# Seven products for all eight pairs of blocks, and one written order for eight batches

## The chip, the core and the metric

One core of a Trainium2 chip. Its engines take their instructions in order, each from its own queue: TensorE (PE; PEld is its weight load), VectorE (DVE), ScalarE (ACT), GpSimd (POOL) and SyncE (SP), which here issues nearly all transfers. The metric is the device time of one execution in microseconds.

## The reference

Two attentions per batch through 32 packed tokens, then a two-layer block with a gate. 8 batches, 8 heads, 576 rows, 64 per head, so 4608 tokens of 512; the hidden size is 2048.

```python
p_packed = sm_attn(p, k, v)             # 32 packed rows against 576 keys
out = sm_attn(q, p_packed, p_packed)    # 576 rows against the 32 packed rows
x = out.transpose(0, 2, 1, 3).reshape(B * S, H * D)
h = x @ w_in
g = h * np.clip(h + 3.0, 0.0, 6.0) / 6.0
return g @ w_out
```

## The kernel before

**Number form.** The large products are made as three matmuls each, of high and low parts in a 32-bit format: high by high, high by low, low by high (`product`, line 967). The low part is the value less its high part, made by a copy on ScalarE and a subtraction (`split`, line 945); `parted` (line 949) does that with the subtraction on GpSimd (line 947).

**First product.** The attention's second step is folded into the first layer: `u_m` multiplies the packed rows of a batch by a quarter of the first layer's weights (`M`, four quarters a batch), and `first_product` (line 922) makes the hidden rows of one of 16 blocks of 128 with six matmuls of 256 or 320 columns. `gate_into` (line 938) applies the gate: ScalarE's addition and cut (line 940), VectorE's minimum and product (line 941). First products use two banks of PSUM in turn (`ps_h`). A batch of 576 rows is two halves of 256 rows and 64 left-over rows, which the wide half (320 columns) keeps in `bnd` (line 965); the left-over rows of two batches make one more group of 128.

**Second product.** A block by itself (a single) is multiplied into both accumulators A and B of a half, three matmuls of 512 columns each. Two blocks together (a pair, `pair_product`) are a 2x2 product of block matrices in seven products instead of eight, 21 matmuls of 256 columns, with four accumulators A to D. The sums that it needs on the row side are made for each half (VectorE, lines 1241, 1249, 1254; parts by `parted`), those on the weight side, `T1` to `T4`, once in batch 1 (`combine`, line 1058). Six of the eight pairs take this form from batch 2 on, four in the second half of batch 1, none before. The combined weights have four places; pairs 0 and 1 share theirs with 4 and 5, and are kept in DRAM and fetched in turn (`fetch_t`, line 1104). After the last pair the four singles follow, and during them the sums of C and D are made (lines 1134 to 1146); the last single closes A and B (line 1153) and the half's two row blocks are stored. Left-over rows of batches 2 and 3 are joined to the singles of a half of batch 3; those of 4 to 7 make a half of their own in batch 7 (`moe_edges`).

**Attention of the next batch** runs in the gaps of the current one: `S` (scores of packed rows against keys, `u_s1`), `E`, `V`, `T`, and `Z` (scores of queries, `u_s2`). A round of scores is eight small matmuls packed into TensorE's array, one bank of PSUM for even and one for odd heads; 576 columns go as two rounds of 288, one after the other (`both_halves`, line 362), since one pair of banks serves the attention. Batch 1 alone has both rounds at once.

**Order.** Batch 0 runs by a list written by hand (`PLAN`): each name is a chain, each mention its next step. From batch 1 on, steps are handed to a planner, which orders them by simulated costs; `fill` (line 1449) hands out the attention's steps behind the gates of the current block, with counts in `STAGES`, `LATE`, `TURN` and `FETCHES`.

Of the kernel before, what the change touches and what calls it, by code (L numbers as in the profile page):

```python
# [18 lines left out]

STAGES = (((0, 1), (6, 2), (19, 2)), ((0, 1), (10, 2), (19, 1)))


LATE = (3, 2, 1, 2, 1)
PAIRS = 6
FIRST_PAIRS = 4
TURN = (
    (5, 5, 6, 6, 7, 7, 7), (7, 8, 8, 9, 9, 9, 10), (10, 10, 11, 11, 12, 12, 12), (13, 13, 13, 14, 14, 15, 15),  # L30
    (27, 27, 28, 28, 28, 29, 29), (29, 29, 30, 30, 30, 31, 31),
)
FETCHES = (((5, 1), (7, 0)), ((5, 4), (7, 5)))

PLAN = """
in in in in lo0 lo2 in in k0 in p li0 k1 in p k0 k2 k1 kr k2 in s0 kr b2 s0 b0 k3 s0 b2 li1 s0 warm b2 s0 in
k3 b2 in b0 s1 s0 li2 q1 b2 e0 q1 c0 s1 b2 e0 q0 c0 li3 s0 s1 v0 q0 s0 s1 s1 v0 b0 lp s1 b0 e1 a0 v0 c1 qr
v0 e1 c1 s1 a0 z0 qr b0 s1 a0 z0 b0 v1 a0 z0a a1 z0a upper a1 z0a lo1 q2 v1 li4 a1 q3 q2 z0a a1 v1 q3 v1 z0a  # L40
z1 z1 li7 a2 m0 z1a a2 m1 a2 z1a a2 lo3 a3 z1b z0a lk0 a3 z1b z1b z0a z1b z0a z1a z0a z1b lo5 z1a b1 li6 z1a
z1b m0 z1b b1 z1a z1a z1b z0a a4 z1a m0 li5 z1b z0a warm a3 z1b z0a m1 m0 z1b a7 lk2 z1a h0 m0 z1a m1 b1 a7
z1a b1 b3 h0 b3 lo4 b3 a3 warm r0 m1 a4 r0 b3 m2 lo8 tp h1 r0 m1 a7 y0 b1 h1 r0 m2 lo6 a4 x0 b1 r1 a4 x0 m2
m2 a6 r1 x0 a6 m2 h2 a7 tk0 r1 h2 y1 a5 lk3 r1 a5 x0 y1 a5 x1 r2 a6 a5 b5 x1 r2 b3 x1 tk2 r2 y0 h3 a6 b4 r2
lk1 h3 b4 b5 m4 x1 b3 r3 b4 li8 b5 m4 b4 li10 r3 x2 li9 m4 m4 x2 lo7 r3 m4 b5 below h4 b4 tk3 y3 b6 h4 b4 y3
lq1 y2 b6 x2 r3 b5 x2 b6 r4 tk1 x3 b6 b8 r4 x3 a8 b5 S a8 x3 a8 r4 y4 a8 S S S S x3 b8 y4 h5 a10 li11 r4 a10
lo9 h5 a10 a9 b8 lq3 x4 b8 r5 x4 b6 r5 S x4 y2 a10 r5 tq1 h6 lo10 b8 r5 lq2 h6 y5 a9 y5 S x4 a9 r6 b8 x5 a9
S b7 S x5 r6 a11 x5 li12 S a11 a11 h7 b6 r6 a11 S h7 r6 x5 b9 r7 li13 m8 S lv b7 b7 x6 r7 y6 b7 m8 x6 y7 r7
# [27 lines left out]
def packed_attention_moe(  # L78
# [97 lines left out]

# [1338 lines left out]
```

## Time and profile before

| | us |
|---|---|
| median of 3 runs | 708.94 |
| lowest, highest | 706.88, 710.05 |
| profiled execution | 709.52 |
| its span, first to last instruction | 707.7 |

Busy time counts an engine's instructions alone; matmuls overlap, so the time of one on the page is longer than the distance to the next. A wait is put down to what ended last. The chain that ended last is, by share of the span, TensorE 82%, VectorE 7%, transfers 5%.

### The profile page before, as it was taken

To read this page: it belongs to the slowest core of one execution; us is meant where nothing else is said; L and a number is where in the kernel's file an instruction comes from. 1 tells how busy PE (TensorE), PEld (TensorE's weight loads), DVE (VectorE), ACT (ScalarE), POOL (GpSimd) and SP (SyncE) were. 2 spreads that over 40 slices of the span, in tenths; PEclk is the share of its full clock that TensorE was granted. 3 is DMA by queue.
4 is the path that set the end of the run, shared out by engine and by line. 5 is a ranking of instruction groups with operands and counts; after the bars stand their busy time and mean duration, and the time that the engine had idled before them with its cause. 6 is when DMAs were issued, how large, how long until landed. Compare 5 with 4: busy or idle time off the path is not lost.

```text
span 707.7 us, 16190 instructions
## 1 busy us (share of the span) xinstructions
PE 684.7 (97%) x5924; PEld 591.9 (84%) x5924; DVE 544.2 (77%) x1227; ACT 428.8 (61%) x1004; POOL 335.9 (47%) x515
## 2 busy tenths in 40 slices
PE   6599999999999999999999999999999999999997
PEld 4477877888879888899898888899888988899997
DVE  2897788788999759877788777877698778867754
ACT  5798876556566646565455655656475755565553
POOL 2475541113425456371272626474453646475552
PEclk9699999999999999999999999999999999999999
DMA  9989852955338655465554647375755644340330
GB/s 277 310 216 240 218 141 88 287 150 116 117 123 208 161 131 210 127 158 108 107 200 125 164 103 232 121 158 129 196 200 143 168 127 150 129 170 1 120 119 30
DMA packets 199679, 111.15 MB, mean 157 GB/s; under 512 B 173489, under 2 KB 185265, under 8 KB 195761
## 3 DMA queue, kind: packets, MB, share of 16 engines
q1 hardware_dynamic: 199056, 109.94, 55.8%
q8 instruction: 46, 0.75, 0.4%
q14 instruction: 33, 0.26, 0.1%
q10 hardware_dynamic: 544, 0.20, 0.1%
HBM read 92.27 MB, written 17.83 MB: 156 GB/s over the span
## 4 chain that ended last, share of the span: by engine, by line
PE 82%; DVE 7%; DMA 5%; issue 2%; SPq 1%; ACT 1%; POOL 1%; DVEq 0%; ACTq 0%; POOLq 0%
PE acc L969 48%; PE ps_hh L929 22%; PE ps L350 5%; PE ps_h L607 3%; DMA w_again<-w_kept 2%; PE ps L470 1%; SPq L294 1%; DMA room<-in_q_dram 1%; PE ps L440 1%; DMA wt<-t_kept 1%; DVE tr L555 1%; DMA p_nat<-in_p_dram 1%; DVE osb L1153 1%; PE ps L273 1%; DVE t L941 0%
## 5 line engine op out<-in xcount | busy, mean ns | idle before, releaser
L929 PE MATMUL ps_hh<-a_hi,m_hi 128*128 128x320 f32 (+1 forms) x448 | 133.5, 298 | 1.0 <-DVE t L941 0.9
L929 PE MATMUL ps_hh<-a_lo,m_hi 128*128 128x320 f32 (+1 forms) x448 | 133.0, 297 | 0.0
L929 PE MATMUL ps_hh<-a_hi,m_lo 128*128 128x320 f32 (+1 forms) x448 | 132.7, 296 | 0.0
L969 PE MATMUL acc<-wo_hi,g 128*128 128x512 f32 x304 | 109.0, 402 | 0.0
L940 ACT ACTIVATE t<-ps_hh,three 128x320 f32<-128x320 f32 (+1 forms) x148 | 73.5, 500 | 47.4 <-PE ps_hh L929 36.0
L941 DVE SCALAR_TENSOR_TENSOR t<-t,ps_hh 128x320 f32<-128x320 f32 (+1 forms) x148 | 65.7, 445 | 45.1 <-ACT t L940 44.4
L947 POOL TENSOR_TENSOR ge<-t,ge 128x256 fp32r<-128x256 f32 x76 | 60.3, 793 | 80.8 <-ACT ge L946 32.1
L929 PEld LDWEIGHTS ps_hh<-a_hi,m_hi 128*128 128x128 f32 x448 | 84.7, 189 | 7.7 <-DVE t L941 2.7
L929 PEld LDWEIGHTS ps_hh<-a_lo,m_hi 128*128 128x128 f32 x448 | 84.7, 189 | 4.8 <-issue 1.9
L929 PEld LDWEIGHTS ps_hh<-a_hi,m_lo 128*128 128x128 f32 x448 | 84.7, 189 | 1.7 <-issue 1.3
L965 POOL COPY bnd<-t 128x64 f32<-128x64 f32 x76 | 24.2, 318 | 120.0 <-DVE t L941 117.8
L969 PE MATMUL acc<-wt,ga 128*128 128x256 f32 x492 | 80.4, 284 | 0.3 <-ACT ga L946 0.2
L969 PE MATMUL acc<-wo_hi,ge 128*128 128x256 f32 x328 | 77.8, 285 | 0.0
L947 POOL TENSOR_TENSOR gf<-tb,gf 128x256 fp32r<-128x256 f32 x76 | 65.0, 855 | 17.5 <-ACT gf L946 14.9
L947 POOL TENSOR_TENSOR ga<-t,ga 128x256 fp32r<-128x256 f32 x76 | 60.8, 800 | 24.4 <-ACT ga L946 24.2
L969 PEld LDWEIGHTS acc<-wo_hi,g 128*128 128x128 f32 x304 | 56.1, 188 | 16.2 <-issue 3.0
L969 PEld LDWEIGHTS acc<-wt,ga 128*128 128x128 f32 x492 | 68.0, 190 | 1.2 <-issue 0.5
L969 PEld LDWEIGHTS acc<-wo_hi,ge 128*128 128x128 f32 x328 | 57.5, 190 | 7.0 <-issue 2.8
L969 PE MATMUL acc<-wo_lo,g 128*128 128x512 f32 x152 | 60.1, 395 | 0.0
L555 DVE STREAM_TRANSPOSE tr<-nat 128x576 f32<-128x576 f32 x56 | 42.4, 765 | 16.7 <-DMA nat<-in_q_dram 10.4
L940 ACT ACTIVATE tb<-ps_hh,three 128x256 f32<-128x256 f32 (+1 forms) x76 | 37.9, 499 | 23.0 <-PE ps_hh L929 18.6
L969 PE MATMUL acc<-wt,gf 128*128 128x256 f32 x246 | 50.1, 283 | 0.3 <-DMA wt<-t_kept 0.3
(234 smaller groups left out, 1780.5 us busy)
## 6 DMA issues: line engine op xcount, KB each, us to landing
w_again<-w_kept SPq DMA_DIRECT2D x24, 1024.0 KB, 4.8
wt<-t_kept SPq DMA_DIRECT2D x26, 768.0 KB, 5.2
out_dram<-osb SPq DMA_DIRECT2D x35, 256.0 KB, 2.4
nat<-in_k_dram SPq DMA_DIRECT2D x112, 72.0 KB, 3.2
nat<-in_q_dram SPq DMA_DIRECT2D x112, 72.0 KB, 2.7
raw_out<-in_moe_w_out_dram SPq DMA_DIRECT2D x10, 512.0 KB, 5.1
raw_in<-in_moe_w_in_dram SPq DMA_DIRECT2D x10, 512.0 KB, 5.6
w_kept<-w_in_sb SPq DMA_DIRECT2D x4, 1024.0 KB, 7.6
```

Of the source, the lines that this page charges most:

```text
L273: nc.tensor.matmul(banks[x][NPK * a:NPK * a + NPK, :n * P], state["pp"][half, NPAIR * x + a], cols[half, :, a], start=True, stop=True,)
L294: nc.sync.dma_start(out=t[r:r + 32], in_=src[b, 2 * a + h, :, 32 * c:32 * c + 32].rearrange("(t i) j -> i t j", i=32),)
L350: nc.tensor.matmul(pair[x][NPK * a:NPK * a + NPK, :n], rows[half, a], c, start=True, stop=True)
L440: nc.tensor.transpose(out=pair[x][:, c * P:(c + 1) * P], in_=e[x][:, c * P:(c + 1) * P], identity=ident)
L555: nc.vector.transpose(out=t, in_=state.pop(("nat", which, b, a)))
L607: nc.tensor.matmul(h[:, hf, :HS], mm[:, g, fs], aa[:, hf * HS:(hf + 1) * HS], start=(g == 0 and i == 0), stop=(g == NG - 1 and i == 2),)
L929: state["first"] = nc.tensor.matmul(h[:, :n], mm[:, g, fs], aa[:, t0:t0 + n], start=(g == 0 and i == 0), stop=(g == NG - 1 and i == 2),)
L940: state["relu"] = nc.scalar.activation(out=t[:, :n], in_=h, func=AF.Relu, bias=three)
L941: state["gate"] = nc.vector.scalar_tensor_tensor(out=t[:, :n], in0=t[:, :n], scalar=6.0, in1=h, op0=ALU.min, op1=ALU.mult)
L947: engine.tensor_sub(out=lo, in0=x, in1=hi.bitcast(F32))
L965: nc.gpsimd.tensor_copy(out=bnd[:, f, side * REM:side * REM + REM], in_=t[:, boff:boff + REM])
L969: nc.tensor.matmul(out, lhs[x], rhs[y], start=first and i == 0, stop=last and i == 2, skip_group_check=True)
```

## The change

- All eight pairs are made by seven products in batches 2 to 7 and in the half of left-over rows. In the first half of a batch they come in the order `DOWN`, in the second in `ORDER`; in batch 1 it stays four pairs. Combined weights of pair 3 and of pair 6 have places of their own, six others share three places, are kept in DRAM and fetched.
- Pair 6's place and a small staging tile take the room of `bnd`. So left-over rows of batches 2 to 6 go to DRAM, two blocks a store, and come back in batch 7, where those of 2 to 5 make a half and those of 6 and 7 a chain of their own.
- Scores from batch 2 on are one round of 512 and 64 columns. The 64 take both banks of the first products. Small transposes that took an accumulator's bank take the attention's.
- Batch 0's loads are chains of their own, and all eight batches run by written lists (`PLANS`), one step of one engine at a mention; `'` and `"` name a step of the batch before or after. Loads stand further ahead of their use, and queries and values ahead of the first output weights.
- In the last half, the sums of C and D and the last additions are cut in pieces of 256 columns on VectorE, each stored as it is made.

In the lists `f` is half of a first product, `g` the gate and the sums behind it, `a` to `d` the parts, `x` one of a pair's seven products, `e` the left-over rows, `r` and `o` the sums and stores of a half, `T` the combining of weights, `ft` a fetch; names with `n` belong to the next batch's attention (`nS`, `nZ` the scores). Shown are the first lines of batches 0 and 1, the lines around the scores in batch 2, and the last lines.

```diff
-LATE = (3, 2, 1, 2, 1)
-PAIRS = 6
...
+PAIRS = 8
 FIRST_PAIRS = 4
...
+ORDER = (1, 0, 2, 3, 5, 4, 6, 7)
+DOWN = (5, 4, 3, 7, 6, 1, 0, 2)
+
+SLOT = {0: 0, 1: 1, 2: 2, 3: 3, 4: 0, 5: 1, 7: 2}
+KEPT = {0: 0, 1: 1, 2: 2, 4: 3, 5: 4, 7: 5}
...
+PLANS = (
+    """
+lp0 lk_0 k0 lkr p p k0 lk_1 k1 k2 k1 s0 k2 lq_1 kr k3 k3 lqr kr s0 s0 s0 li0 lq_0 a0 a0 s0 s0 warm a0 s1 s1 q1
+s1 s1 s1 s1 e0 e0 c0 c0 q0 lv_0 v0 q1 q0 s0 s0 v0 s1 s1 e1 v0 c1 c1 lq_2 v0 qr qr a0 z0 z0 z0a z0a z0a li1 a1 e1
+q2 lv_1 a1 z0a z0a a1 a1 v1 v1 lq_3 q3 v1 v1 z0a q2 q3 z1 z1 z0a m0 z0a z0a lo2 b2 lo0 li2 b2 m0 upper z1b lp
...
+f00 'y14 f00 g00 'o1 nlk0 ntk0 M1 g00 nlk1 'x14 p00 p00 f01 f01 M2 M2 ntk1 M2 g01 g01 M2 f02 M2 ntp 'x15 f02 p01
+x00 e00 g02 g02 e01 p01 f03 p02 p02 nlk2 nlk3 f03 g03 g03 M3 T0 ntk2 ntk3 e03 p03 T0 x01 f04 j01 'o0 T0 M3 M3
...
+f05 f05 nlk3 f04 g01 d01 g04 d01 g03 c03 M3 x01 x01 x01 g03 c03 x01 a02 x03 x03 x01 g04 f06 M3 M3 f06 'T6 x03
+g05 g05 x03 x03 x03 d03 ntk3 g04 g06 g06 g05 c05 g05 a04 b05 d03 'T6 g06 nS nS nS f07 f07 b05 x05 x05 nS x03 a06
...
+d1d d1d f1f f1f x1b g1e x1b g1f g1f x1d x1b g1f g1f c1d d1b x1d x1d x1d o20 a1e a1e b1f b1f x1f ft12 x1f x1f x1f
+c1f c1f x1b x1d x1d d1f d1f x1b x1f x1f r1 x1d r1 x1f o10 r1 r1 o10 r1 o11 o10 o10 o11 o11
...
+def written(ch):
+
+    for b, plan in enumerate(PLANS):
+        for name in plan.split():
+            near = {"'": b - 1, '"': b + 1}.get(name[0])
+            yield (b, name) if near is None else (near, name[1:])
...
     def att_ps():
-        return spare_ps(0) if steady else ps_a.tile([P, 512], F32, name="ps1", tag="att")
+        return att_pair()[0] if steady else ps_a.tile([P, 512], F32, name="ps1", tag="att")
...
     def spare_pair():
         if steady:
-            return [spare_ps(x) for x in range(2)]
+            return [ps_h.tile([P, 512], F32, name="ps_s", tag="h") for _ in range(2)]
...
+    def all_rows(b, lhs, rhs):
+
+        cuts = (slice(0, HS), slice(HS, S)) if b == 1 else (slice(0, NB), slice(NB, S))
+
+        def cols(cut):
+            return lambda a, half: rhs[a][half].rearrange("p t i -> p (t i)")[:, cut]
+
+        done = each_head(lhs, *(cols(cut) for cut in cuts))
+        yield None
+        for n in (1, 0):
+            yield n, cuts[n], [ps[:, :cuts[n].stop - cuts[n].start] for ps in done[n]]
...
-        for part in both_halves(b == 1, pt, kt):
+        for part in all_rows(b, pt, kt):
...
-        for part in both_halves(not roles, pps[b % 2], qt):
+        for part in all_rows(b, pps[b % 2], qt):
...
+        if i == 6:
+            t6 = ep.tile([P, 3, 2, H2], F32R, name="wt6", tag="bnd0")
+            for k, name in enumerate(("T1", "T2", "T4")):
+                blocks[i, name] = [t6[:, k, x] for x in range(2)]
+            x, y = (stage8().rearrange("p f n -> p (f n)")[:, k * H2:(k + 1) * H2] for k in range(2))
...
+        if i in KEPT:
+            nc.sync.dma_start(out=t_kept[KEPT[i]], in_=slots[SLOT[i]].rearrange("p a x m -> p (a x m)"))
+            yield
+
+    def fetch_t(i):
+        nc.sync.dma_start(out=slots[SLOT[i]].rearrange("p a x m -> p (a x m)"), in_=t_kept[KEPT[i]])
...
+    def steps_of(b, c):
+
+        pairs = list(range(FIRST_PAIRS) if b == 1 else DOWN if c == 0 or b == LAST else ORDER)
+        return pairs, [2 * i + k for i in pairs for k in range(2)] + [
+            f for f in range(NF) if f // 2 not in pairs
+        ]
...
+    def keep_edge(b, keep, f, boff, side):
+
+        cols = slice(side * REM, side * REM + REM)
+        if b == 1:
+            place = bnd_at(f, 1)[:, 0, cols]
+        elif b == LAST:
+            place = parked["last"][f // 4][:, f % 4, cols]
+        else:
+            place = stage8()[:, f % 8]
+        nc.gpsimd.tensor_copy(out=place, in_=keep["t"][:, boff:boff + REM])
+        yield
+        if 1 < b < LAST and f % 2:
+            two = slice(f - 1, f + 1)
+            nc.sync.dma_start(out=e_kept[b // 2, :, two, cols], in_=stage8()[:, f % 8 - 1:f % 8 + 1])
+            yield
...
                     bank(x)[:, half * H2:half * H2 + H2], lhs[l], block(i, r), fresh,
-                    i == pairs[-1] and x in "CD",
+                    i == pairs[-1] and (x in "CD" or not singles),
...
+        def summed():
+
+            sixth = 1.0 / 6.0
+            r1, r2 = made["r"] = [gp.tile([P, DM], F32, name="osb") for _ in range(2)]
+            nc.scalar.activation(out=r1, in_=bank("C"), func=AF.Copy, scale=sixth)
+            yield
+            u1 = r2[:, H2:]
+            (nc.vector if end else nc.gpsimd).tensor_tensor(out=u1, in0=r1[:, :H2], in1=r1[:, H2:], op=ALU.add)
+            yield
...
+        def finished(k):
+            r = made["r"][k]
+            for cut in ((slice(0, H2), slice(H2, DM)), (slice(H2, DM), slice(0, H2)))[k] if end else (slice(0, DM),):
+                own = cut if k == 0 or singles else slice(cut.start, min(cut.stop, H2))
+                if own.start < own.stop:
                     nc.vector.scalar_tensor_tensor(
-                        out=dst, in0=bank("D")[:, half * H2:half * H2 + H2], scalar=sixth, in1=other,
-                        op0=ALU.mult, op1=ALU.add,
+                        out=r[:, own], in0=bank("AB"[k])[:, own], scalar=1.0 / 6.0, in1=r[:, own], op0=ALU.mult, op1=ALU.add
                     )
-
-                added(r1[:, H2:], 0, u1)
-                added(r2[:, :H2], 1, u1)
-                added(r2[:, H2:], 0, r2[:, :H2])
...
-        for name in PLAN.split():
+        for b, name in written(ch):
```

## Rows read from the trace of the kernel before

**Rows 1.** The page: busy time of each engine over the span, and TensorE's busy share and granted clock in 40 equal slices.

```profile
PE 684.7 (97%) x5924; PEld 591.9 (84%) x5924; DVE 544.2 (77%) x1227; ACT 428.8 (61%) x1004; POOL 335.9 (47%) x515
...
PE   6599999999999999999999999999999999999997
...
PEclk9699999999999999999999999999999999999999
```

**Rows 2.** TensorE's own waits over the whole span: what waited for what, us in total, times, the longest.

```profile
PE ps_t L886 <- DVE m_lo L286: 5.3, 1, 5.3
...
PE ps_w L803 <- issue: 2.0, 1, 2.0
...
PE ps_hh L929 <- DVE t L941: 0.9, 2, 0.5
PE ps L350 <- DMA w_again<-w_kept: 0.8, 1, 0.8
```

**Rows 3.** The timeline of TensorE at 400 to 412 us: start, duration, operation. Between the first two lines lie eleven starts of the same shape, between the last two three of 512 columns.

```profile
400.74 0.28 PE L929 MATMUL ps_hh<-a_hi,m_hi 128*128 128x256 f32 x1
...
402.18 0.28 PE L969 MATMUL acc<-wo_hi,gf 128*128 128x256 f32 x1
...
410.64 0.39 PE L969 MATMUL acc<-wo_hi,g 128*128 128x512 f32 x1
...
411.57 0.28 PE L929 MATMUL ps_hh<-a_hi,m_hi 128*128 128x256 f32 x1
```

**Rows 4.** The timeline of TensorE around score rounds: two rounds together in batch 1, a single round of a later batch, and a packed step of batch 0 with 32 columns.

```profile
10.04 0.30 PE L731 MATMUL ps_w<-room 64*32 64x32 f32 x16
...
55.85 0.39 PE L969 MATMUL acc<-wo_hi,gl 128*128 128x512 f32 x1
56.17 0.71 PE L350 MATMUL ps_w<-tr,p_tr 64*32 64x288 f32 x16
56.68 0.69 PE L350 MATMUL ps<-tr,p_tr 64*32 64x288 f32 x16
...
57.64 0.40 PE L969 MATMUL acc<-wo_lo,gh 128*128 128x512 f32 x1
...
476.41 0.31 PE L929 MATMUL ps_hh<-a_lo,m_hi 128*128 128x320 f32 x1
...
477.00 0.31 PE L929 MATMUL ps_hh<-a_hi,m_lo 128*128 128x320 f32 x1
477.24 0.71 PE L350 MATMUL ps<-tr,p_tr 64*32 64x288 f32 x16
...
478.11 0.28 PE L969 MATMUL acc<-wo_lo,gf 128*128 128x256 f32 x1
```

**Rows 5.** The timeline of all engines near the end: the last matmul of the last first product, and the end of its gate on VectorE (it comes by ScalarE, line 940).

```profile
699.39 0.28 PE L929 MATMUL ps_hh<-a_hi,m_lo 128*128 128x256 f32 x1
...
700.28 0.42 DVE L941 SCALAR_TENSOR_TENSOR t<-t,ps_hh 128x256 f32<-128x256 f32 x1 [0.37 <-ACT t L940]
```

**Rows 6.** Groups by line and shape on VectorE (busy us, mean ns, idle before); then two lines' operations with their shortest, median and longest duration in ns; the subtractions of line 947 on VectorE and GpSimd over the span; and two stretches with the busy time of each engine.

```profile
L1249 DVE TENSOR_TENSOR t<-t,tb 128x256 f32<-128x256 f32 x76 | 43.5, 572 | 1.5
...
L1254 DVE TENSOR_TENSOR tb<-tb,t 128x128 f32<-128x128 f32 x76 | 36.8, 484 | 1.6
...
L947 DVE TENSOR_TENSOR g<-t,g 128x256 fp32r<-128x256 f32 x72 | 30.1, 423 | 6.4 <-ACT g L946 4.7 <-PE acc L969 0.5
...
L1241 DVE TENSOR_TENSOR t<-t 128x128 f32<-128x128 f32 x76 | 24.6, 323 | 1.9
...
L1249 DVE TENSOR_TENSOR t<-t,tb x76: 400/426/965, 174.5 to 691.9; 128x256 f32<-128x256 f32 x76
...
L941 DVE SCALAR_TENSOR_TENSOR t<-t,ps_hh x148: 374/442/489, 121.5 to 700.3; 128x320 f32<-128x320 f32 x76, 128x256 f32<-128x256 f32 x72
...
0.00:708.00 708.00, 41.03 (x102) 227.62 (x322) 0.99 0.56 157
...
180.00:200.00 20.00, 18.85 (x163) 14.97 (x162) 19.03 (x40) 11.98 (x29) 9.56 (x13) 1.00 0.19 68
...
240.00:260.00 20.00, 20.00 (x217) 17.90 (x216) 13.88 (x39) 12.14 (x30) 7.78 (x14) 1.00 0.58 136
```

**Rows 7.** One stretch of the start with the busy time of each engine, granted clock, share of the DMA engines and GB/s; and the transfers that SyncE issued at the start.

```profile
20.00:40.00 20.00, 11.28 (x133) 8.51 (x133) 16.58 (x40) 14.52 (x30) 11.60 (x10) 0.66 1.08 295
...
1.77 0.50 SPq L176 DMA_DIRECT2D raw_out<-in_moe_w_out_dram  x1
2.31 0.60 SPq L176 DMA_DIRECT2D raw<-in_moe_w_out_dram  x1
...
4.79 0.90 SPq L643 DMA_DIRECT2D room<-in_q_dram  x2
```

**Rows 8.** The timeline of all engines at the end: the last two additions and the last matmul; and the copy of a bank that stands ahead of the sums, by shape.

```profile
703.22 1.39 DVE L1153 SCALAR_TENSOR_TENSOR osb<-acc,osb 128x512 f32<-128x512 f32 x2 [1.62 <-PE acc L969]
...
703.48 0.39 PE L969 MATMUL acc<-wo_hi,g 128*128 128x512 f32 x1
...
L1134 ACT ACTIVATE osb<-acc 128x512 f32<-128x512 f32 x14 | 8.4, 597 | 2.1 <-PE acc L969 2.0
```

**Rows 9.** SyncE's queue: its longest wait on a load of the attention inputs (in total, times, longest); and the page's line of block fetches (count, KB each, us to landing).

```profile
SPq L294 <- DVE tr L555: 67.2, 12, 8.8
...
wt<-t_kept SPq DMA_DIRECT2D x26, 768.0 KB, 5.2
```

More of the change, by code (lines that the diff above doesn't have):

```diff
@@ L44 @@
[L44 to L48, printed above, removed]
@@ L1109, in sums_of @@
+    def sums_of(ch, b, c, pairs, singles, rows):
         banks, made = {}, {}
+        end = (b, c) == (LAST, 1)
         def bank(x):
@@ L1127, in pair_product @@
                     bank(x)[:, half * H2:half * H2 + H2], lhs[l], block(i, r), fresh,
[L1128 removed]
+                    i == pairs[-1] and (x in "CD" or not singles),
                 )
[L1130 to L1138 removed]
+                yield
@@ new lines, in single_products @@
+        def single_products(f, keep):
+            g = keep["g"]
+            for k, x in enumerate("AB"):
+                second_product(
+                    f, bank(x), g[:, k * P:(k + 1) * P], g[:, (2 + k) * P:(3 + k) * P],
+                    first=False, last=f == singles[-1],
+                )
+                yield
+        def finished(k):
[3 more added lines that the diff above has]
+                if own.start < own.stop:
@@ L1204, in moe_pairs, with pairs_half @@
+                nc.sync.dma_start(out=rows[k][:, cut], in_=r[:, cut])
+                yield
+        ch[b, f"r{c}"] = summed()
+        for k in range(2):
+            ch[b, f"o{c}{k}"] = finished(k)
+        return pair_products, single_products
+    def pairs_half(ch, b, c):
+        pairs, steps = steps_of(b, c)
         even = b % 2 == 0
@@ L1284, in moe_pairs, with gate_even @@
-        if joined:
-            pend[-1:-1] = edges
+        pair_products, single_products = sums_of(
+            ch, b, c, pairs, steps[2 * len(pairs):], [out[row + k * P:row + (k + 1) * P] for k in range(2)]
+        )
+        def gate_even(keep):
+            ta = keep["t"] = gp.tile([P, WT], F32, name="t")
+            yield from gate_into(ta, keep, n)
+            a1, a2 = (ta[:, off + k * P:off + (k + 1) * P] for k in range(2))
+            nc.vector.tensor_sub(out=ta[:, W + off:W + off + P], in0=a2, in1=a1)
+            yield
@@ new lines, in last_edges, with acc, parts, products @@
+    def last_edges(ch, b):
+        banks = []
+        def acc():
+            if not banks:
+                banks.append(acc_of(roles[3]))
+            return banks[0]
+        for f in range(0, NF, 2):
+            summed, keep = f // 2 in ORDER, {}
+            def parts(f=f, summed=summed, keep=keep):
+                yield from edge_parts(edge_rows("last", f, 2), summed, keep)
+            def products(f=f, summed=summed, keep=keep):
+                yield from edge_product(acc, f, *keep["j"], summed, f == 0, f == NF - 2)
+            ch[b, f"j3{f:x}"] = parts()
+            ch[b, f"y3{f:x}"] = products()
+        ch[b, "o30"] = stored(acc, out[b * S - REM:b * S + REM], dict(tag="g", bufs=4))
@@ L1490, in packed_attention_moe @@
-            if (b, c) == (FOUR + 3, 0):
-                moe_edges(kept.pop("eb"), [out[x * S - REM:x * S + REM] for x in (FOUR + 1, FOUR + 3)])
-        if b == 1:
-            rest(*turned)
-    with tc.manual_schedule(engines={mybir.EngineType.PE}):
-        second(0)
+                next(ch[b, name])
 _INS = ['q', 'k', 'v', 'p', 'moe_w_in', 'moe_w_out']
```

1005 lines of the change are left out of this document (554 added, 451 removed).

## The prediction

> **What bounds the kernel now.** I read the busy line of the page first: TensorE is busy for 97% of the span, VectorE for 77%, ScalarE 61%, GpSimd 47%; the slices show TensorE's holes in the first two and a last partial one only [rows 1]. A busy TensorE is not yet a full one, so the list of its waits comes next: what is long (5.3 and 2.0 us) lies in the first 40 us, and after that the longest entries are 0.9 and 0.8 us in total [rows 2]. Last, the timeline at two quiet places, for the distance between starts, which is the real price of a matmul, where the mean duration is not (matmuls overlap): twelve matmuls of 256 columns start within 1.44 us, 0.120 us each; four of 512 within 0.93 us, 0.2325 us each [rows 3]. So from 40 us on the end moves only with the number and width of matmuls, and elementwise work, loads and stores count only where they make TensorE late.
>
> **Seven products for all eight pairs.** By the code, a pair is 21 matmuls of 256 columns, and its two blocks as singles are 2x2x3 = 12 of 512. In batches 2 to 7 (12 halves), and in the half made of leftover rows, two pairs each go from the second form to the first: 13 x 42 = 546 more of 256, 13 x 24 = 312 fewer of 512. In the other leftover chain two pairs more are summed: +12 of 256, -6 of 512. Together +558 x 0.120 = +67.0 us, -318 x 0.2325 = -73.9 us [rows 3]: **-7.0 us**. Batches 0 and 1 keep their forms. It pays while a 256 costs under 318/558 = 0.57 of a 512; the rows say 0.516, so only about a tenth of that matmul time is saved. The Trainium skill (TensorE: Matmul & The Clock Gate, Back-to-back issue gap) gives a sustained spacing of about 131 ns at 512 columns and 81 ns at 128; by a line between them the edit would cost some 13 us. The row is 0.2325 us at 512, in full stream and at full clock, so the trace disagrees, and that case gets a chance of 0.01 below.
>
> **Whole-row scores in one round.** Now each of the two score steps of batches 2 to 7 (12 in all) runs as two rounds of 288 columns. A round costs, from where the next matmul would have started to where the stream goes on (the second start after it less its spacing): from 477.00 + 0.147 to 478.11 - 0.12, 0.84 us (0.147 is the spacing of the 320-column matmuls); two are 1.68. Batch 1 already issues two together: from 55.85 + 0.23 to 57.64 - 0.23, 1.33 us [rows 4]. One entry and one exit go. The new rounds, 512 and 64 columns, have the same 576, so 1.33 again if columns set the price; the 64-column part should be 64/288 of the 0.49 that a second round adds, 0.11, but sixteen instructions of even 32 columns take 0.30 [rows 4], so up to 0.19 more. 12 x 0.35 = 4.2 us at best, 12 x 0.16 = 1.9 at worst; I take **-3.6**, near the row of two rounds together, which has the same form.
>
> **The banks it borrows.** The 64 columns go into the two banks that first products use. So a round now waits until both last first products are gated, and the next first product waits until the 64 columns are read. From the end of a first product (699.39 + 0.12) to the end of its gate on VectorE (700.28 + 0.42) is 1.19 us [rows 5]; the readers are two short operations on each of two banks, bounded above by about 0.5 us. Uncovered, that is 1.7 us a round, 20 us in all; covered, 0. The new list puts three to seven products (0.36 us each) between the last first product and the round, and the 512-column part hides the readers in part. I take a quarter of a microsecond each, **+3.0**. The small transposes that leave the accumulator banks for the attention pair's bank are in it: what is queued behind them on TensorE is the product stream.
>
> **One written order.** The waits of TensorE after 40 us that an order can move are the 0.9 and 0.8 in the rows and a few smaller ones [rows 2], some 3 us. A fixed list can remove them and can make its own: I take half, **-1.6**, bounds -3.3 and +3. On SyncE's queue the loads stand earlier; a load whose buffer is still being read holds the stores and fetches behind it, as now [rows 9]. Fetches of combined blocks go from 26 to 39 (counted in the list), 768 KB and 5.2 us to landing each [rows 9], and 40 small stores of leftover rows come in. In the list a slot's fetch stands four to five pairs of some 4 us ahead of its use: 0, and if that cover is gone, some 5 us once per fetch.
>
> **The first 40 us.** TensorE is busy for 11.3 of the 20 us from 20 on, with the DMA engines at 1.08 of their time at 295 GB/s, and the clock in that stretch averages 0.66 between its two levels [rows 7]. Two loads of 512 KB of output weights (1.77 and 2.31 us) stand before queries and values now; the list moves them behind the last query. 1.05 MB at 295 GB/s is 3.6 us earlier for the queries, if they set the pace: the 2.0 us wait is in their region [rows 2, 7]. But the chain of softmax steps on VectorE behind them, which ends in the 5.3 us wait, is as long as before. **-2.0**, bounds -3.6 and +1 (weights late by as much as the order shifts them).
>
> **Combined blocks for two more pairs.** By the code, each takes some 11 VectorE operations of 256 columns; with 0.42 to 0.57 us each [rows 6], 10 us more, once, in batch 1 and early in batch 2. VectorE is at 19.03 of 20 us from 180 on and at 13.88 from 240 on [rows 6]: they fit in the second stretch, and are costed at 0; were all in the first, +10.
>
> **Elementwise work of pairs.** 26 blocks' pairs more. On VectorE each adds 0.323 + 0.572 + 0.484 us and saves two splits of 0.423: +13.9 us in all. On GpSimd 76 pairs and the small half take 227.6 us in these subtractions, 2.8 a pair: +73 us [rows 6], so GpSimd goes from 47% to about 59%, VectorE to 81%. Neither is the bound: 0. What speaks against it: VectorE's additions with both operands in SBUF take 400 ns at least, 426 median and 965 at most, while its gate, with one operand in PSUM, stays between 374 and 489 [rows 6]. The Trainium skill (SBUF: State Buffer, Who interferes with whom) says that GpSimd and VectorE share a port pair that one holds for a whole instruction, the other blocked. By that rule the rows are read easily, and more GpSimd subtractions mean more stretched additions on the way to a pair's product. It is a rival below, priced from rows.
>
> **The last stores.** Now TensorE's last slot ends at 703.71, two additions end at 704.61, and the span ends at 707.7 [rows 8]: 4.0 us. With no singles left, the last pair closes the sums itself: after the last product of bank C, one copy of 0.60 us and seven pieces on VectorE of 0.35 us (half of 0.69) [rows 8], 3.2 us with one hand-over, of which 0.72 lies beside the last two products. So 2.5 us between TensorE's end and the last addition where 0.9 are now: +1.6; halved stores can give a little back. **+1.5**, bounds 0 and +2.
>
> **Sum**, against the profiled execution of 709.5 us (span 707.7 and 1.8 around it): -7.0 - 3.6 + 3.0 - 1.6 - 2.0 + 1.5 = -9.7, so 699.8. The median of the runs shown is 708.9, 0.6 below that execution: **699.2 us**.
>
> **Rivals.**
> (A) Everything hides: no borrowed-bank waits, all old waits gone, the loads' full gain, no longer tail: -7.0 - 4.2 - 3.3 - 3.6 = -18.1, which with the 0.6 is 690.8 us. For it: nearly every wait of TensorE now is under 1 us [rows 2], so a list can be this good. Against it: the tail is longer by the code, and the banks are shared by the code.
> (B) VectorE and GpSimd become late: each of the 26 pairs makes TensorE wait for its last part. A stretched addition costs 965 - 426 = 0.54 us [rows 6]; 0.4 a pair are 10.4 us and eat the gain: about 709 us, no change. For it: the stretched rows, and GpSimd's share. Against it: products stand a pair behind their parts, 2.5 us of products as cover.
> (C) Slower, one mechanism: the borrowed banks. If a round waits for the whole 1.7 us, 20.4 us stand in place of 3.0: 699.2 + 17.4 = 716.6 us. It decides from about 1.4 us a round on (slower by over 0.5%). Against it: three to seven products are in the list ahead of each.
> (D) The wider matmul was the cheap one (the page's spacing): slower too; by rows it would need 256 columns at more than 0.57 of 512, against 0.516.
>
> **Chances.** Forecast, 695 to 705.3: 0.59. A, 690 to 695: 0.15. B, within 0.5%: 0.17. C 0.08, D 0.01. A measurement of this kernel can tell about 0.5%, 3.5 us. Faster 0.74, same 0.17, slower 0.09. The range leaves out the lowest end of A and the far end of B and all of C: 692 to 708.5. The forecast's own range is 695 to 705.3.
>
> **What would show it.** Products: 558 more starts of 256 and 318 fewer of 512, at 0.120 and 0.2325 us; another spacing makes the first term wrong. Scores: groups of 32 records once per step, about 1.35 us; a hole before or behind them beyond 0.5 us is C. B would show as waits of TensorE for GpSimd's or VectorE's parts inside halves of batches 2 to 7, and a mean of the two-operand additions above 0.60 us. Loads: the query transposes of the second half start before 20 us. Tail: over 5 us from TensorE's last slot to the end. Waits on fetched blocks beyond 1 us in total would make the order's term wrong, and a hole around 190 to 230 us the combined blocks'.

## The result, and the profile after

The changed kernel takes **713.48 us** (median of 8 runs, 711.08 to 716.08) beside 708.43 (8 runs of before): ratio 1.0073 [1.0048, 1.0099]. It is slower by 0.7%, where 1.4% faster was forecast. The profiled execution of after is 715.55 us (span 713.8), 6.0 over that of before; the prediction's sum said 9.7 under it.

The page of after: busy time of each engine; then the two kinds of transfer that move the most bytes.

```profile
PE 682.9 (96%) x6164; PEld 604.1 (85%) x6164; DVE 557.2 (78%) x1281; ACT 433.2 (61%) x1062; POOL 390.5 (55%) x620
...
wt<-t_kept SPq DMA_DIRECT2D x39, 768.0 KB, 5.3
w_again<-w_kept SPq DMA_DIRECT2D x24, 1024.0 KB, 5.5
```

TensorE is busy for 1.8 us less than before [rows 1] while the span is 6.1 longer, so the time in which it stands grew. (Busy time hides short stops: a matmul of 256 columns counts with 0.28 us in it, and the next one can start after 0.120.) VectorE and GpSimd came out a little under where they were put (78% and 55%; forecast 81% and 59%).

The timeline of TensorE in after: from the first line to the second are six spacings of 256 columns, then comes a score round.

```profile
400.82 0.28 PE L1120 MATMUL ps_hh<-a_hi,m_hi 128*128 128x256 f32 x1
...
401.54 0.28 PE L1120 MATMUL ps_hh<-a_hi,m_hi 128*128 128x256 f32 x1
...
417.13 0.28 PE L1011 MATMUL acc<-wo_hi,gf 128*128 128x256 f32 x1
417.34 0.34 PE L488 MATMUL ps_s<-tr,pps 64*32 64x64 f32 x16
417.48 1.06 PE L488 MATMUL ps<-tr,pps 64*32 64x512 f32 x16
418.52 0.41 PE L1120 MATMUL ps_hh<-a_hi,m_hi 128*128 128x320 f32 x1
418.77 0.30 PE L1120 MATMUL ps_hh<-a_lo,m_hi 128*128 128x320 f32 x1
```

0.72/6 is 0.120 us, as in [rows 3]. The round costs, by the way of counting of the prediction, from 417.13 + 0.12 to 418.77 - 0.147, 1.37 us, where two rounds cost 1.68 [rows 4]: -3.7 us in twelve. Counted the same way one by one, the twelve cost 1.32 to 1.69 us each, 16.4 in all, and the 24 of before 20.1. Both gains are there.

TensorE's waits in after, the whole span (what waited for what; us in total, times, longest):

```profile
PE ps_h L688 <- ACT a_hi L960: 5.8, 1, 5.8
PE ps_t L768 <- DMA k_nat<-in_k_dram: 5.1, 1, 5.1
PE acc L1011 <- DMA wt<-t_kept: 2.9, 2, 2.6
PE ps L488 <- DMA w_again<-w_kept: 1.5, 2, 1.1
...
PE ps L601 <- DMA v_high<-in_v_dram: 1.1, 2, 0.6
PE acc L1011 <- POOL ge L1142: 1.1, 1, 1.1
...
PE acc L1011 <- POOL ga L1142: 0.9, 2, 0.6
PE ps L488 <- DVE osb L1284: 0.6, 1, 0.6
PE acc L1011 <- ACT ga L1140: 0.5, 1, 0.5
...
PE acc L1011 <- DVE osb L1284: 0.5, 1, 0.5
...
PE ps_hh L1120 <- DVE mx L518: 0.3, 1, 0.3
```

The first two lie in the first 40 us. They answer to the 5.3 of [rows 2] and to a wait for the keys at the very start that [rows 2] and the prediction leave out:

```profile
PE ps_t L678 <- DMA k_nat<-in_k_dram: 5.2, 1, 5.2
```

Behind 40 us the list puts 5.5 us on transfers (a fetched block, W_in read again, values), where before had 1.1, 2.5 on the parts of pairs (before 0.7) and 0.5 on accumulators still being read out. The 0.6 of L488, put down to VectorE's `osb`, stands ahead of a product with W_in, and by its times it is a wait for W_in too: the load was asked for at 333.84 us and landed 8.4 us later, and the product starts at 342.42. That makes 6.1 for transfers. The wait for the banks that the score round borrows, which had a term of +3.0, is the 0.3 of the last line and little more.

Where the longest of the new ones comes from: SyncE's queue in after, 253 to 281 us (start, us, instruction), and its longest wait in that stretch.

```profile
253.49 0.34 SPq L1651 DMA_DIRECT2D w_again<-w_kept  x1
...
254.36 4.03 SPq L434 DMA_DIRECT2D nat<-in_k_dram  x4
269.04 0.35 SPq L1651 DMA_DIRECT2D w_again<-w_kept  x1
...
269.93 4.21 SPq L434 DMA_DIRECT2D nat<-in_k_dram  x4
274.23 1.65 SPq L1314 DMA_DIRECT2D out_dram<-osb  x2
275.93 0.42 SPq L1094 DMA_DIRECT2D wt<-t_kept  x1
```

```profile
SPq L1651 <- PE ps L488: 10.5, 1, 10.5
```

SyncE issues nothing from 258.4 to 269: the load of the next chunk of W_in has one buffer, which TensorE still has to read. Behind it in the same queue stand loads, stores, and the fetch of a combined block, asked for at 275.93 and needed at 277.9. What that does to TensorE, and the granted clock (last number but two) in the two stretches:

```profile
277.88 0.31 PE L1120 MATMUL ps_hh<-a_hi,m_lo 128*128 128x320 f32 x1
280.78 1.01 PE L1011 MATMUL acc<-wt,gf 128*128 128x256 f32 x3 [2.60 <-DMA wt<-t_kept]
281.59 0.41 PE L1011 MATMUL acc<-wo_hi,ge 128*128 128x256 f32 x1
281.80 0.41 PE L1011 MATMUL acc<-wo_lo,ge 128*128 128x256 f32 x1
```

```profile
278.00:280.70 2.70, 0.19 (x2) 0.00 (x0) 2.60 (x9) 1.22 (x3) 1.41 (x3) 0.97 1.05 293
280.70:284.00 3.30, 3.22 (x14) 3.22 (x15) 1.10 (x2) 0.41 (x1) 0.73 (x1) 0.50 0.97 254
```

After the stop the clock is at its lower level (0.50 of 2.4 GHz) for 3.3 us, and 256 columns start 0.21 us apart: the 14 matmuls in it would take 1.8 us at the spacings of full clock (0.120, and 0.147 for 320 columns), so some 1.5 come on top of the wait.

The end of after (all engines), to be held against [rows 8]:

```profile
705.25 0.40 ACT L1140 CAST ga<-t 128x256 fp32r<-128x256 f32 x1 [4.07 <-PE acc L1011]
...
706.52 0.74 PE L1011 MATMUL acc<-wt,ga 128*128 128x256 f32 x4 [0.31 <-POOL ga L1142]
...
707.69 0.28 PE L1011 MATMUL acc<-wo_hi,ga 128*128 128x256 f32 x1
707.93 0.42 DVE L1280 TENSOR_TENSOR osb<-osb 128x256 f32<-128x256 f32 x1 [5.56 <-ACT osb L1277]
...
709.90 0.75 DVE L1310 SCALAR_TENSOR_TENSOR osb<-acc,osb 128x256 f32<-128x256 f32 x2
```

The last slot ends at 707.81, the additions at 710.65, the span at 713.8: 2.8 us of VectorE behind TensorE where 0.9 were, 6.0 us of tail for 4.0. Ahead of it TensorE stands for 1.2 us (by its starts) for the last pair's parts, whose buffer is held until 705.2 by the pair before.

### The profile page after: what moved, and what is told of

Same layout as the page of the kernel before. It is cut to its first block, busy times and chain, and to the rows that moved or that the text cites. A ratio compares the mean times of both kernels' runs of the same rounds, so it can differ in the third digit from the quotient of the medians.

```text
span 713.8 us, 17016 instructions
## 1 busy us (share of the span) xinstructions
PE 682.9 (96%) x6164; PEld 604.1 (85%) x6164; DVE 557.2 (78%) x1281; ACT 433.2 (61%) x1062; POOL 390.5 (55%) x620
## 4 chain that ended last, share of the span: by engine, by line
PE 78%; DVE 9%; DMA 6%; ACT 2%; issue 2%; POOL 2%; SPq 1%; DVEq 0%; ACTq 0%; POOLq 0%
PE acc L1011 43%; PE ps_hh L1120 22%; PE ps L488 4%; PE ps_h L688 3%; DMA w_again<-w_kept 2%; PE ps L601 1%; DMA raw_in<-in_moe_w_in_dram 1%; DMA wt<-t_kept 1%; PE ps_t L768 1%; DVE osb L1284 1%; DMA t_kept<-wt 1%; DVE t L1134 1%; PE ps L571 1%; SPq L434 1%; DVE z L625 1%
## 5 line engine op out<-in xcount | busy, mean ns | idle before, releaser
L1120 PE MATMUL ps_hh<-a_hi,m_hi 128*128 128x256 f32 (+1 forms) x448 | 136.9, 306 | 1.0 <-DVE mx L518 0.3
L1120 PE MATMUL ps_hh<-a_hi,m_lo 128*128 128x256 f32 (+1 forms) x448 | 132.7, 296 | 0.0
L1120 PE MATMUL ps_hh<-a_lo,m_hi 128*128 128x256 f32 (+1 forms) x448 | 132.6, 296 | 0.0
L1011 PE MATMUL acc<-wo_hi,ge 128*128 128x256 f32 x432 | 105.7, 286 | 1.4 <-POOL ge L1142 1.1
L1011 PE MATMUL acc<-wt,ga 128*128 128x256 f32 x648 | 102.0, 284 | 0.8 <-ACT ga L1140 0.5
L1134 DVE SCALAR_TENSOR_TENSOR t<-t,ps_hh 128x320 f32<-128x320 f32 (+1 forms) x124 | 55.4, 448 | 39.1 <-ACT t L1132 38.4
L1142 POOL TENSOR_TENSOR ga<-tb,ga 128x128 fp32r<-128x128 f32 x100 | 49.9, 499 | 35.4 <-ACT ga L1140 30.6
L1134 DVE SCALAR_TENSOR_TENSOR tb<-tb,ps_hh 128x256 f32<-128x256 f32 (+1 forms) x100 | 44.4, 446 | 26.8 <-ACT tb L1132 26.5
L1140 ACT CAST ga<-t 128x256 fp32r<-128x256 f32 x100 | 40.1, 404 | 36.2 <-PE acc L1011 27.0
L1011 PE MATMUL acc<-wo_lo,ge 128*128 128x256 f32 x216 | 60.7, 281 | 0.0
L1140 ACT CAST ge<-t 128x256 fp32r<-128x256 f32 x100 | 40.4, 404 | 26.6 <-DVE t L1340 19.7
```

Of the source, the lines that this page charges most:

```text
L1011: nc.tensor.matmul(out, lhs[x], rhs[y], start=first and i == 0, stop=last and i == 2, skip_group_check=True)
L1120: nc.tensor.matmul(h[:, :n], mm[:, g, fs], aa[:, t0:t0 + n], start=(g == 0 and i == 0), stop=(g == NG - 1 and i == 2),)
L1134: nc.vector.scalar_tensor_tensor(out=t[:, :n], in0=t[:, :n], scalar=6.0, in1=h, op0=ALU.min, op1=ALU.mult)
L1140: nc.scalar.copy(out=hi, in_=x)
L1142: engine.tensor_sub(out=lo, in0=x, in1=hi.bitcast(F32))
```

## The experiments

Ratios are to the kernel before, in runs on the same chip. The theory that I set out with, after the traces: the gains are there, and transfers asked for on one in-order queue eat them. Its rivals: the form itself (pairs without single chunks beside them), and the borrowed banks.

**Fetches left out, or asked for at once.** x2 leaves every fetch step out of the list; x1 puts each right behind the last step of the product that frees its buffer.

```diff
-def written(ch):
+def listed(ch):
...
+def written(ch):
+    return [x for x in listed(ch) if x[1][:2] != "ft"]
```

In x2 products read whatever blocks lie in the buffers; in x1 one fetch of batch 2 comes ahead of the store that keeps pair 5's blocks, so that pair reads those of pair 1 from then on.

> The changed kernel without the 39 fetches (it leaves them out, so shared places hold the blocks of another pair; all else runs). Theory 1: the same as with the fetches moved, within 2 us, near 709 to 710. Theory 3: clearly less than with the fetches moved, by 5 us or more, since 30 MB of transfers go, near 705. Theory 2: no change, near 713.

> The changed kernel with each of the 39 fetches of combined blocks named right behind the last product that frees its place, so that no attention load, weight load or store that still waits stands ahead of it on SyncE's queue. Theory 1 (the list is to blame: fetches stand behind waiting loads and stores): the waits for fetched blocks (2.8 and 0.5 us in the profile of the changed kernel) go, about 3 us less than the changed kernel, near 710. Theory 2 (the seven-product form makes the parts late on VectorE and GpSimd): no change, near 713. Theory 3 (more bytes slow every transfer): no change, near 713.

x2: 709.06 us, 1.0011 [0.9998, 1.0024]; x1: 762.12, 1.0764 [1.0746, 1.0782]. The 39 fetches cost 4.4 us, and without them the kernel is still no faster than before. Earlier is no cure: in x1 SyncE stands for TensorE at the fetches and W_in comes late; its longest sums of waits, TensorE's and then SyncE's:

```profile
PE ps L512 <- DMA w_again<-w_kept: 28.1, 7, 6.6
```

```profile
SPq L1118 <- PE acc L1035: 138.2, 28, 21.3
```

**The parts of the change alone, in the planner's order of before.** x3: eight pairs in each half (pairs 6 and 7 read the blocks of 2 and 3); x5: seven pairs, with their own blocks; x4: one score round of 512 and 64 columns, in the banks of the first products (the first lines of the diff are x3's, the last x4's).

```diff
-PAIRS = 6
+PAIRS = 8
...
-            return [spare_ps(x) for x in range(2)]
+            return [ps_h.tile([P, 512], F32, name="ps_s", tag="h") for _ in range(2)]
```

> The kernel before, in its own planned order, with all eight pairs by seven products in batches 2 to 7 and in the half of left-over rows (pairs 6 and 7 use the combined blocks of pairs 2 and 3: it leaves out the combining of two more pairs and the 13 more fetches). Theory 1: the form gives what its matmuls say, 7 us less, perhaps 2 lost at the ends of halves: 701 to 704. Theory 2: the gain is eaten by late parts: 708 or more.

> The kernel before, in the planner's order, with one more pair of chunks: seven pairs and two single chunks in each half, nothing else of the change. The matmul term of the prediction was -7.0 us for two more pairs, so -3.5 us for one, and one more block per half is fetched (13 more fetches of 768 KB). Theory 'order': the form itself brings what the pitches say and only the order of the steps takes it back; then the planner's own order with seven pairs comes out at 704 to 706 us, 3 us under the kernel before. Rival 'form': fewer single chunks leave less other work in which the accumulators are emptied and blocks are fetched, whatever the order; then it comes out at 708 to 713 us.

> The kernel before with whole-row scores in one round of 512 and 64 columns for batches 2 to 7, the 64 in the first products' banks; six pairs, planned order. Twelve rounds at 1.33 in place of 1.68 us are 4.2 us less: 704 to 705 if the banks cost nothing. If the banks cost TensorE as much as one uncovered gate a round (1.2 us), 12 x 0.85 us more: 718.

x3: 716.96 us, 1.0133 [1.0112, 1.0154]; x5: 720.81, 1.0158 [1.0137, 1.018]; x4: 729.54, 1.0307 [1.0288, 1.0326]. No part pays by itself under the planner. x3 waits for W_in and for accumulators; x5's loss is for the most part one wait, for a gate that stands on VectorE behind eleven steps of one block's combining (217 to 223 us):

```profile
PE ps L351 <- DMA w_again<-w_kept: 2.9, 2, 2.5
PE acc L970 <- ACT osb L1135: 2.1, 1, 2.1
```

```profile
PE ps_hh L930 <- DVE tb L942: 6.5, 1, 6.5
```

So x3 and x5 don't tell the form from its order: each has its own accident of order. x4 has the size of rival C (20.4 us), but its trace names only 4.4 us as waits for gates of first products, so C's mechanism is not shown by it; in the written list the cost is not there. Nor is its round the one of the change: in eleven of its twelve rounds the planner lets two of the 32 matmuls go ahead of the other 30, with other products between, and the twelve cost 21.9 us, more than the 20.1 of before.

**The last stores.** x6 has them in one piece again.

```diff
-            for cut in ((slice(0, H2), slice(H2, DM)), (slice(H2, DM), slice(0, H2)))[k] if end else (slice(0, DM),):
+            for cut in (slice(0, DM),):
```

> The changed kernel with each of its last two 128-row stores in one piece, as before, and nothing else. Theory: the pieces are worth little, and the tail of 6.0 us behind the last product (4.0 us before) comes from work that is still to do on VectorE and ScalarE when the last product ends: two of the four last steps now wait for a product's end; then this is 713 to 715 us, 0 to 1.5 us over the changed kernel. Rival: cutting the stores adds issues of some 0.5 us each to the end; then it is 711.5 to 712.5 us, 1 to 2 us under it.

717.35 us, 1.0112 [1.0092, 1.0133], over both ranges that were set down. The end does not explain it: from the last product's start to the end are 6.13 us, with pieces 6.07. The difference lies 200 us and more ahead of the edit, in waits for fetches and W_in (3.7 and 2.6 us in this run). Why these fall otherwise in a program that is the same up to there stays open; it shows how far they move the time by themselves.

**One load in its turn.** In batch 2, w1 stands 59 steps ahead of the product that frees its buffer; x7 puts it right behind.

```diff
-x0f g14 f16 r0 r0 r0 r0 f16 b13 "nlk0 x11 g15 w1 f17 f17 o00 e12 x11 o01 g14 x11 g13 a12 c13 d13 x11 nT b13 x13
+x0f g14 f16 r0 r0 r0 r0 f16 b13 "nlk0 x11 g15 f17 f17 o00 e12 x11 o01 g14 x11 g13 a12 c13 d13 x11 nT b13 x13
...
-x13 f18 x15 f19 f19 "ntk0 b17 c15 x13 e14 b17 x17 nZ d15 g17 nM2 nZ nZ d15 g19 g19 a14 c15 g18 g18 x15 c17 a16
+x13 f18 x15 f19 f19 "ntk0 b17 c15 x13 e14 b17 x17 nZ d15 g17 nM2 w1 nZ nZ d15 g19 g19 a14 c15 g18 g18 x15 c17 a16
```

> The changed kernel with one step of its list moved: in batch 2 the load w1 stands behind the first step of nM2, whose matmuls free its buffer, and no longer 59 steps ahead of it. Theory 'queue': SyncE's queue, which stood from 258 to 269 us at this load with the fetches and loads behind it, goes on working, the wait of 2.8 us for a fetched block at 278 us and the 0.5 us at 285 us go, and about 2.6 us at 283 us (the same stall in the run without fetches) does not take their place: 709.5 to 711.5 us. Rival 'order of use': the fetches stand in the list behind the first use of their blocks, so TensorE waits for them wherever the queue stands: 712.5 to 714 us.

712.29 us, 1.0053 [1.0034, 1.0073]: within error of after. The 10.5 us stand of SyncE became 5.3, the fetch behind it was issued at 269.3 and not 275.9, but took 10.1 us to land among loads and stores asked for around the same time, and TensorE still stood for it, 2.2 us.

**Earlier in the list, or on a second queue.** x9 moves nine fetches 8 to 86 steps ahead (and puts w1 in turn); x8 has all fetches issued by ScalarE at their places, x12 by ScalarE 12 steps behind the freeing product (the first three of batch 2 at their old places; w1 in turn), x14 and x15 have W_in issued by ScalarE, three of its four chunks right behind ScalarE's first copy of the product that frees the buffer, x15 with the nine fetches ahead. The diff shows the queues: the first two lines are of x8 and x12, the last two of x14 and x15.

```diff
-        nc.sync.dma_start(out=slots[SLOT[i]].rearrange("p a x m -> p (a x m)"), in_=t_kept[KEPT[i]])
+        nc.scalar.dma_start(out=slots[SLOT[i]].rearrange("p a x m -> p (a x m)"), in_=t_kept[KEPT[i]])
...
-        nc.sync.dma_start(out=t.rearrange("p f a e -> p (f a e)"), in_=w_kept[n])
+        nc.scalar.dma_start(out=t.rearrange("p f a e -> p (f a e)"), in_=w_kept[n])
```

> The changed kernel with the load w1 of batch 2 behind the first step of nM2, and nine fetches of batches 2 to 4 (the three of each second half), which stood at or a few steps from the first use of their blocks, 20 to 60 steps earlier in the list, each still some steps behind the product that frees its buffer. Theory 'place in the list': the fetches are late because they are written late; the waits for fetched blocks (2.2 us in the run with w1 moved alone) go to under 0.5 us, and the time to 709.5 to 711.5 us. Rival 'the queue stands': SyncE now waits at each fetch for TensorE to free the block, and the loads behind it are late instead, as in the run with each fetch right behind its product: 714 to 725 us.

> The changed kernel with its 39 fetches asked for by ScalarE at the same places of the list, so that nothing on SyncE's queue can hold them up. Theory 'queue': the fetches come some microseconds earlier, the loads behind them on SyncE's queue too: 708.5 to 711 us, near the 709.1 us of the run without fetches. Rival: ScalarE, which drains the first products, stands at a fetch until TensorE has freed the block, and each stand delays a gate: 714 to 720 us.

> The changed kernel with w1 of batch 2 in turn, and the fetches asked for by ScalarE, each 12 steps of the list behind the product that frees its buffer (the first three of batch 2 at their old places). Theory 'one queue': the fetches hold up nothing on SyncE, and on ScalarE they stand far enough ahead of use: TensorE's waits for fetched blocks and for W_in go, 706 to 709 us. Rival 'the transfers collide': both kinds are still asked for within the same few microseconds and land late: 711 to 715 us. Second rival: ScalarE stands at the fetches and delays the gates, as when they stood late in the list: 716 us and more.

> The changed kernel with W_in's chunks that are read again (w1, w0, w3 of each batch) asked for by ScalarE, each right behind ScalarE's first copy of the product that frees the buffer, and w2 at its place, by ScalarE too; the fetches stay on SyncE at their places. Theory 'one queue': SyncE no longer stands for TensorE at a W_in load, the fetches behind it come earlier, and W_in lands earlier in the list than it did: 708 to 711 us. Rival: the fetches are written at the first use of their blocks and stay late: 712 to 714 us.

> The run beside it with the nine fetches of batches 2 to 4 moved 20 to 60 steps ahead on SyncE, as in the earlier run where W_in then came late by 3.4, 2.7 and 2.3 us. Theory 'one queue': W_in no longer stands behind them, both waits are gone: 706 to 709 us. Rival 'the transfers collide': W_in lands late all the same and the time is 712 to 717 us.

x9: 717.08, 1.0121 [1.0105, 1.0137]; x8: 748.45, 1.0568 [1.0536, 1.0601]; x12: 714.24, 1.0076 [1.0049, 1.0103]; x14: 741.73, 1.045 [1.0424, 1.0475]; x15: 739.07, 1.04 [1.0365, 1.0436]. In x9 no wait for a block is left, and W_in, behind them, is late three times; the low clock makes the stop dearer (a round of 1.09 us takes 1.96):

```profile
PE ps L488 <- DMA w_again<-w_kept: 8.1, 3, 3.4
```

```profile
284.12 1.96 PE L488 MATMUL ps<-w_again,pps 64*32 64x512 f32 x16 [3.42 <-DMA w_again<-w_kept]
```

x8 shows that the places in the list are late ones: ScalarE, which goes through the list at its pace, asks too late nine times (28.4 us), where SyncE makes up for it by running ahead. x12, with places ahead, has no wait for a block, and in their stead these:

```profile
PE ps L515 <- DMA w_again<-w_kept: 3.8, 2, 2.2
PE ps L515 <- DVE tb L1389: 1.7, 1, 1.7
...
PE ps L515 <- DVE t L1382: 1.2, 1, 1.2
```

The last two are put down to VectorE's sums, but by their times they are waits for W_in as well: those loads, asked for at 425.51 and 511.65 us, landed after 9.0 and 8.3 us (the median in after is 5.5), and what reads them starts at 434.63 and 520.09. So W_in makes 6.7 us of waits. 'One queue' as the whole cause fell: with two queues the time is the same, inside the range of the rival 'the transfers collide'. That rival is not shown by it alone, since x12 also moved the places. x14 and x15 tell less than they were meant to: w2 too went to ScalarE at its old place, late, and made waits of up to 6.2 us.

**The late parts, and both.** x10 gives the last pair's third parts buffers of their own and moves some parts to VectorE; x11 is x9 and x10.

```diff
+            room = own() if last and c == 1 else third(lhs)
...
-                yield from parted(lhs, ("A11", "A12"), t, edge_rows(js[0], 2 * i, 2))
+                yield from parted(lhs, ("A11", "A12"), t, edge_rows(js[0], 2 * i, 2), nc.vector)
```

> The changed kernel with the parts that TensorE waits for in batch 7 made earlier: the last pair's third parts get buffers of their own (those of the edge rows, free by then), so that they no longer wait for the pair before to be multiplied; the fourth part of the first half's last pair, the sum of its two halves and one part of each left-over pair are made on VectorE and not on GpSimd. Theory: TensorE's waits of 0.76, 0.72 and 1.24 us at 641 to 658 us and 0.70 and 0.47 us at 705 to 706 us go, 2.5 to 3.9 us in all: 709.5 to 711 us. Rival: TensorE is held a little later by the next step of the same chain (the accumulators, the casts on ScalarE), and at most 1 us is won: 712.5 to 713.5 us.

> Both edits of the two runs beside it. If the changed kernel's time is its matmuls and score rounds as predicted plus these waits, the two gains add up: 706 to 708.5 us, under the kernel before for the first time. If the waits only move from one place to the next, it is 710 to 713 us.

714.38, 1.0081 [1.0058, 1.0105], and 716.83, 1.0132 [1.0111, 1.0154]. The waits of 1.2 us at 705 us went; the move to VectorE made those around 641 to 674 us longer (1.5 and 1.5 for its parts, where GpSimd's were 0.6 and 1.1), and they cancel.

**The sum.** x13 is x12 with the last pair's own buffers, x17 is after with w1 in turn and those buffers, and x16 is x17 without its fetches.

> The run beside it (fetches by ScalarE, 12 steps behind the freeing product), and in batch 7 the last pair's third parts in buffers of their own, nothing moved to VectorE. Theory: TensorE's waits of 0.70 and 0.47 us at the end go, as they did in the run on late parts, and this is 0.7 to 1.2 us under the run beside it. Rival: the same as the run beside it within 0.5 us, since the accumulators' reading out sets the end.

> The same two edits with the fetches kept, the layer as in the reference. From the two edits alone (w1 in turn: 712.3 us; the last pair's buffers: 1.2 us of waits) it should be 710.5 to 712 us, still over the kernel before, since the fetches' cost of some 4 us stays. Rival: 713 us and more, if the 1.2 us at the end come back as waits for the accumulators.

> The changed kernel without its 39 fetches (the products then read the blocks that lie in the buffers, so what is summed is not the layer), with w1 of batch 2 in turn and the last pair's third parts in buffers of their own. Theory 'the named waits are the loss': the run without fetches (709.1 us) less its wait of 2.5 us for W_in at 283 us and less the 1.2 us at the end: 705 to 706.5 us. Rival 'waits only move': 707.5 to 709 us.

x13: 712.18, 1.0049 [1.0031, 1.0067], 2 us under x12 with intervals that overlap; x17: 714.41 (710.14 to 716.46), 1.0075 [1.0047, 1.0103]; x16: **705.37** (704.02 to 705.78), **0.9958 [0.9945, 0.9971]**. x16 is what the named waits predicted: two mends worth 3.7 us by the trace, 3.7 us under x2. To the tenth that is luck: x2's runs spread over 4.4 us, and the clock was at its lower level for 3.4 us behind its wait for W_in, which the price leaves out. x17, the same with fetches, is 9 us above it, as slow as after, and its runs scatter over 6.3 us where x16's keep within 1.8. The longest of TensorE's waits in x16 behind the first 40 us, in which it stands for 5.8 and 5.2 as in after:

```profile
PE acc L1016 <- POOL ge L1147: 1.1, 1, 1.1
PE acc L1016 <- POOL ga L1147: 0.6, 1, 0.6
```

No version that computes the layer beat the kernel before. Six of the seventeen times lie in a range set down ahead of the run (x2, x3, x9, x12, x16, x17); the others were not foreseen, most of them slower than every theory named.

## Why the prediction was wrong

- **Pairs, -7.0: right.** The starts are 0.120 us apart as in [rows 3], and their number is as counted: 2316 of 256 columns and 408 of 512, before 1758 and 726. In x16, where transfers hold nothing up, second products run from 39.1 to 696.1 us, 657.0 us, before from 40.5 to 703.5, 663.0: 6.0 us less, where this term and the next should give 10.7. So the matmuls and rounds are won, but 4.7 us of new stops go against them even without fetches, 1.7 of them late parts by the list. D (another spacing) is out.
- **Scores, -3.6: right**, -3.7 by the twelve rounds; 1.37 is near the 1.33 of two rounds together.
- **Borrowed banks, +3.0: too dear.** 0.3 us and a few tenths in the list, which the 16.4 us of the rounds hold already. C did not occur there.
- **One written order, -1.6 (bounds -3.3 to +3): this step failed**, in the sentence "In the list a slot's fetch stands four to five pairs of some 4 us ahead of its use: 0". I had counted pairs between the freeing and the use, not where the fetch stands: in batches 2 to 4 several fetches are written right at the first product that reads them, or a few steps behind it, and what decides is when SyncE gets to them. The clause that followed, 5 us per fetch without cover, was priced and not carried into the range. The clause "a load whose buffer is still being read holds the stores and fetches behind it, as now" named a mechanism and let it pass at nothing. It was 10.5 us of standing at one load, against 26 fetches that TensorE never had to wait long for before. In all the fetches cost 4.4 us (x2), or 9 where the rest is mended (x16, x17): waits for blocks, for W_in and values behind them, and the low clock after a stop; W_in's late load in batch 2 costs 2.5 even without fetches. That the standing of the queue is the way in which they cost it is not shown: with it halved (x7) or with two queues (x12) the time stayed. A slower kernel had a chance of 0.09, for the borrowed banks and another spacing; it was neither.
- **First 40 us, -2.0: about half won.** Second products start at 41.4 us in the profiled run of after, 40.5 before. But that run is the latest of its kind: in the profiles of the fourteen other kernels with the same start they begin at 39.0 to 40.6 us, 39.3 in the middle, and at 40.5 to 40.7 in the four with the start of before. The DMA engines are busy there all the time, as in [rows 7], and the two long waits stayed; the 2.0 us one is not in after's list. After's stretch, as there:

```profile
20.00:41.00 21.00, 12.00 (x189) 8.93 (x188) 17.09 (x39) 16.10 (x34) 12.83 (x11) 0.84 1.02 284
```

- **Combined blocks, 0: right for after**, no stop over 0.4 us between 180 and 230 us; x5 shows the other end, 6.5 us.
- **Elementwise, 0: about 3 us short.** Rival B is right only in batch 7, where the cover of a pair's products is missing (2.5 us of waits for parts and 0.5 for accumulators). The rule of the Trainium skill that was weighed there (SBUF: State Buffer, Who interferes with whom) made nothing worse here: VectorE's two-operand additions take 499 ns in the mean, 100 of them, and 572, 76 of them, before [rows 6].
- **Tail, +1.5: +2.0**, by the VectorE work that was counted.

The sum with these in place, against the profiled run of before: -7.0 - 3.7 (the banks' waits in it) + 0.9 (start) + 2.0 (tail) + 3.0 (parts, accumulators) + 6.1 (transfers) + 1.5 (clock after the 2.6 us stop) = +2.8 of +6.1. Of this, before had 1.8 us of the same waits itself, so some 5 us are not named by the lists. They count a wait from 0.28 us behind the last start, where the next could come after 0.120: each is 0.16 longer than listed, and stops under that are not listed. By the distances between starts, the stretch from the first second product to the last (41.35 to 707.69 us, before 40.46 to 703.48) is 3.3 us longer where 10.7 were won, so stops grew by 14.0: 5.9 for transfers, 1.5 by the low clock, 2.6 for batch 7's parts and accumulators, and some 4 in short stops of up to 0.4 us each, whose causes stay open. Such stops stand in x16 too, and with no fetch at all it is still 6.2 us over the forecast of 699.2.

What stays open: whether any order serves both kinds of transfer in time. Blocks have three buffers and W_in one, both are asked for as TensorE frees them, and in every order tried with the fetches kept TensorE waited for one or the other. A second buffer for W_in was not tried.

The Trainium skill (DMA: Bandwidth & Descriptors, Issuing engines are not separate DMA queues) says that starting transfers from several engines only saves the issuing engine's own time, since they share the same DMA engines. x12 agrees in its result, 714.2 us with two queues and 713.5 with one. An issue takes 0.4 us here; SyncE's longest standing at a load of W_in was 10.5 us.

## What to carry to other kernels

When work is cut by a few per cent on an engine that is already 97% busy, price the added transfers by where they stand in the issuing queue: for each, what stands ahead of it, which of these waits for a buffer, and when the engine that frees it gets there. Leaving a kind of transfer out (x2, x16) tells at once what it costs; moving it tells only where the wait goes next. A price given for "if the cover is gone" belongs in the range unless a row excludes it.

## What the runs showed of the hardware

A stop of TensorE of 2.6 us was followed by 3.3 us at the lower level of its clock (granted 0.50, 1.2 of 2.4 GHz), one of 3.4 us (x9) by a round of 1.96 us in place of 1.09. The landing time of a 768 KB fetch, 5.3 us in the median, rose to 10.1 us when it was asked for 1.3 us behind a 1 MB load, right behind two stores of 256 KB and ahead of four loads of 72 KB (x7); that of a 1 MB load, 5.5 us in the median, rose to 8.3 and 9.0 us in x12.
